# Chunks of every third channel, 4,096 accumulated elements and later first transposes in a dynamic convolution with an MoE layer behind it

## The chip, the cores and the metric

The kernel runs on one core of a Trainium2 chip. The metric is the device time of one launch in microseconds: the median of three runs is 808.31 us (807.36 to 809.03). The engines are TensorE (PE, with its weight loads listed as PEld), VectorE (DVE), ScalarE (ACT), GpSimd (POOL) and SyncE (SP). Transfers are issued from SP's queue or from POOL's and run on the core's 16 DMA engines.

## The reference

A dynamic depthwise convolution over time is followed by two matrix products with h - tanh(h) between them.

```
w   = softmax(weight_gen over its last axis)          # [8, 4096, 8 heads, 7 taps]
out[b, s, h, g] = sum_k w[b, s, h, k] * x_pad[b, s + k, h, g]    # 192 channels = 8 heads x 24, 6 zeros ahead
x   = out.reshape(32768, 192)
h   = x @ w_in            # 192 x 2048
g   = h - tanh(h)
y   = g @ w_out           # 2048 x 192
```

All inputs and the output are float32; the matrix products are made in bf16 with float32 sums.

## The kernel before, in words

The 32,768 tokens are cut into 32 blocks (`NTOT`) of 1,024 tokens: 128 partitions with `J` = 8 neighbouring tokens each. Each block goes through these steps.

- `load(n)`, on SP's queue: the weights `wg_t` of the block and `x_t`, which holds 14 rows of 192 channels per partition (8 tokens and the 6 ahead of them). `x_t` has two buffers, so the load waits until the products of block n-2 have read theirs.
- `softmax_exp` on ACT (`e_t`), `softmax_norm` on DVE (`zsum`, `zr`), and at the head of `products(n)` a multiplication on POOL (`wsm`, line 137).
- `products(n)` (line 153): for each tap k = 0 to 6 one multiplication of `x_t[:, k:k+8]` with the tap's weight, 1,536 elements per partition, float32 in and bf16 out. Taps 0, 2, 4 go to the three parts of `even`, taps 1, 3, 5 to those of `odd`, tap 6 to `last`. They run on POOL, but for those that `on_vector` names, which run on DVE. The 24 channels of a head are cut into `NC` = 3 chunks of 8 neighbouring channels; the result stands chunk by chunk, [chunk, token, head, channel], while x is read as it lies, so the output is written in runs of 8.
- After tap 5 POOL issues a DMA (line 161) that adds all of `odd` to `even`, 4,608 elements per partition. `even`, `odd` and `last` have two buffers each.
- `conv(n, chunks)` (line 182): PE transposes and sums: for each chunk, the three parts of `even` and `last` are multiplied with the identity and added up in PSUM (`pc`). Every operand is a pair of tokens, 64 rows by 128 columns, so one of the four groups takes 8 matmuls per chunk. ACT copies the sum to `convT` (line 192).
- `gemm1(n, f)` (line 205) for 16 tiles f of the 2,048 hidden columns: six matmuls into `ph`; ACT makes `th` = tanh (line 214), DVE makes `gt` = ph - th in bf16 (line 216). `ph` and `pc` share three PSUM buffers.
- `gemm2(i)` (line 236): 32 matmuls for one column of 128 tokens, copied by ACT to `out_sb` (line 261); eight of them make a block, which SP stores. It runs one block behind `gemm1`.

The order on every engine is the program's own; nothing is rescheduled (`tc.manual_schedule()`). The main loop takes block n and eight pairs p of hidden tiles. Ahead of the pairs it issues `load(n + 3)` and `products(n + 2)`; in each pair come two `gemm1`, one `gemm2` of block n-1 and, in two of the pairs, the transposes of block n+1: after pair 2 chunks 0 and 1, after pair 5 chunk 2 (in block 0 after pairs 5 and 6). Ahead of the loop stand block 0's load, w_in, products of block 0 (DVE has taps 1, 3, 5, 6), load and products of block 1 (DVE has 2 and 5) and block 0's transposes.

`w_in` is kept in SBUF as [128, 3 chunks, 2048] in bf16 with the same 64 rows in both halves of the partitions; row h*8+g of chunk c is channel h*24 + c*8 + g. It comes in eight DMAs on POOL's queue, one per head, into partitions 0 to 63 (line 305), and a DMA on SP's queue copies these to partitions 64 to 127 (line 312). POOL's queue also loads `w_out` (line 314).

Of the kernel before, what the change touches and what calls it, by code (L numbers as in the profile page):

```python
# [16 lines left out]
def kernel(  # L17
# [8 lines left out]
    nc = tc.nc  # L26

    B, S, D = x.shape
    H, K = weight_gen.shape[2], weight_gen.shape[3]
    G = D // H  # L30
    F = moe_w_in.shape[1]
    P = nc.NUM_PARTITIONS
    R = P // 2
    HALO = K - 1

    J = 8
    TOK = P * J
    JH = J // 2
# [3 lines left out]
    NFT = F // P  # L42
    NC = D // R
    GC = G // NC
    NPAIR = K // 2
    assert S % TOK == 0 and D % R == 0 and H * GC == R and F % P == 0
    assert NFT == 2 * J, "one token block of the second matmul per pair of f tiles"

# [11 lines left out]
    ident = const.tile([P, P], BF16, name="ident")  # L60
# [8 lines left out]
    prods_of = {}  # L69
# [4 lines left out]
    def load(n):  # L74
        b, s = divmod(n, NSB)
        s0 = s * TOK
        wg_t = wgpool.tile([P, J, H, K], FP32, name="wg_t")
        nc.sync.dma_start(
            out=wg_t[:],
            in_=weight_gen[b, s0 : s0 + TOK].rearrange("(p j) h k -> p j h k", p=P),  # L80
        )

        x_t = xpool.tile([P, HALO + J, D], FP32, name="x_t")

        def rows(p0, p1):
            win = x[b, s0 + p0 * J - HALO : s0 + p0 * J - HALO + 1]
            nc.sync.dma_start(
                out=x_t[p0:p1, :, :],
                in_=bass.AP(
                    tensor=win.tensor,  # L90
                    offset=win.offset,
                    ap=[[J * D, p1 - p0], [D, HALO + J], [1, D]],
                ),
            )

        if s == 0:
            nc.sync.dma_start(
                out=x_t[0:1, 0:HALO, :],
                in_=zero[:].rearrange("o (h d) -> o h d", h=1).to_broadcast([1, HALO, D]),
            )  # L100
            nc.sync.dma_start(
                out=x_t[0:1, HALO : HALO + J, :],
                in_=x[b, 0:J].rearrange("(p j) d -> p j d", p=1),
            )

            rows(1, 16)
            rows(16, P)
        else:
            rows(0, P)
        wg_of[n] = wg_t  # L110
        x_of[n] = x_t

    def softmax_exp(n):
        wg_t = wg_of.pop(n)
        e_t = wgpool.tile([P, J, H, K], FP32, name="e_t")
        nc.scalar.activation(  # L116
            out=e_t[:].rearrange("p j h k -> p (j h k)"),
            in_=wg_t[:].rearrange("p j h k -> p (j h k)"),
            func=ACT.Exp,
        )  # L120
        e_of[n] = e_t

    def softmax_norm(n):
        e_t = e_of.pop(n)
        zsum = wgpool.tile([P, J * H], FP32, name="zsum")
        nc.vector.reduce_sum(  # L126
            out=zsum[:], in_=e_t[:].rearrange("p j h k -> p (j h) k"), axis=AX.X
        )
        zr = wgpool.tile([P, J * H], FP32, name="zr")
        nc.vector.reciprocal(zr[:], zsum[:])  # L130
        zr_of[n] = (e_t, zr)

    def products(n, on_vector=()):
        x_t = x_of.pop(n)
        e_t, zr = zr_of.pop(n)
        wsm = wgpool.tile([P, J, H, K], FP32, name="wsm")
        nc.gpsimd.tensor_mul(  # L137
            wsm[:].rearrange("p j h k -> p (j h) k"),
            e_t[:].rearrange("p j h k -> p (j h) k"),
            zr[:].rearrange("p (n o) -> p n o", o=1).to_broadcast([P, J * H, K]),  # L140
        )

        even = ppool.tile([P, NPAIR, NC, J, H, GC], BF16, name="even")
        odd = ppool.tile([P, NPAIR, NC, J, H, GC], BF16, name="odd")
        last = ppool.tile([P, NC, J, H, GC], BF16, name="last")
        dst = {}
        for i in range(NPAIR):
            dst[2 * i] = even[:, i]
            dst[2 * i + 1] = odd[:, i]
        dst[K - 1] = last[:]  # L150
        for k in range(K):
            eng = nc.vector if k in on_vector else nc.gpsimd
            eng.tensor_mul(  # L153
                dst[k].rearrange("p c j h g -> p j h c g"),
                x_t[:, k : k + J, :].rearrange("p j (h c g) -> p j h c g", h=H, c=NC),
                wsm[:, :, :, k : k + 1]
                .rearrange("p j h (k o) -> p j h k o", o=1)
                .to_broadcast([P, J, H, NC, GC]),
            )
            if k == K - 2:  # L160
                nc.gpsimd.dma_start(  # L161
                    out=even[:].rearrange("p i c j h g -> p (i c j h g)"),
                    in_=odd[:].rearrange("p i c j h g -> p (i c j h g)"),
                    accum_op=mybir.AluOpType.add,
                    max_dma_last_dim=3072,
                )
        prods_of[n] = [even[:, i] for i in range(NPAIR)] + [last[:]]

    def conv(n, chunks):

        prods = prods_of[n]
        if n not in conv_of:
            conv_of[n] = cpool.tile([P, NC, HT], BF16, name="convT")
        convT = conv_of[n]
        nch = len(chunks)
        pc = psum_h.tile([P, 2, HT], FP32, name="pc", tag="ph")
        for k in range(NPAIR + 1):
            for ci, c in enumerate(chunks):
                for j in range(JH):
                    col = (ci * JH + j) * R  # L180
                    for r in range(2):
                        nc.tensor.matmul(  # L182
                            pc[:, r, col : col + R],
                            lhsT=prods[k][r * R : (r + 1) * R, c, 2 * j : 2 * j + 2].rearrange(
                                "p j h g -> p (j h g)"
                            ),
                            rhs=ident[r * R : (r + 1) * R, r * R : (r + 1) * R],
                            start=(k == 0 and ci == 0 and j == 0),
                            stop=(k == NPAIR and ci == nch - 1 and j == JH - 1),
                        )  # L190
        c0 = chunks[0]
        nc.scalar.activation(  # L192
            out=convT[:, c0 : c0 + nch, :].rearrange("p c (j r t) -> p r (c j) t", r=2, t=R),
            in_=pc[:, :, 0 : nch * JH * R].rearrange("p r (cj t) -> p r cj t", t=R),
            func=ACT.Copy,
        )
        if c0 + nch == NC:
            prods_of.pop(n)
# [99 lines left out]
    w_in = const.tile([P, NC, F], BF16, name="w_in")  # L298
    w_out = const.tile([P, NFT, D], BF16, name="w_out")

    ctx.enter_context(tc.manual_schedule())

    load(0)
    for h in range(H):
        nc.gpsimd.dma_start(
            out=w_in[h * GC : (h + 1) * GC],
            in_=moe_w_in[h * G : (h + 1) * G].rearrange("(c g) f -> g c f", c=NC),
        )
    softmax_exp(0)
    softmax_norm(0)  # L310
    products(0, on_vector=(1, 3, 5, 6))
    nc.sync.dma_start(out=w_in[R:P], in_=w_in[0:R])
    load(1)
    nc.gpsimd.dma_start(out=w_out[:], in_=moe_w_out.rearrange("(c p) e -> p c e", c=NFT))
    softmax_exp(1)
    softmax_norm(1)
    conv(0, (0, 1))
    conv(0, (2,))
    products(1, on_vector=(2, 5))
    load(2)  # L320
    softmax_exp(2)
    softmax_norm(2)
    for n in range(NTOT):
        if n + 3 < NTOT:
            load(n + 3)
        if n + 2 < NTOT:
            products(n + 2)
        for p in range(J):
            gemm1(n, 2 * p)
            gemm1(n, 2 * p + 1)  # L330
            if p == 1 and n + 3 < NTOT:
                softmax_exp(n + 3)
            if n >= 1:
                gemm2((n - 1) * J + p)
            if n + 1 < NTOT:
                if p == (2 if n else 5):
                    conv(n + 1, (0, 1))
                if p == (5 if n else 6):
                    conv(n + 1, (2,))
            if p == 2 and n + 3 < NTOT:  # L340
                softmax_norm(n + 3)
# [33 lines left out]
```

The softmax here doesn't subtract the row's maximum and nothing guards it: scores larger than these inputs give would overflow.

## Time and profile before

The profiled execution took 807.62 us, of which the span from the first to the last instruction is 805.8 us; the median of the runs is 808.31 us. The granted TensorE clock was 0.997.

| engine | busy us | share of the span | instructions |
|---|---|---|---|
| PE | 737.1 | 91% | 14,336 |
| POOL | 713.0 | 88% | 297 |
| DVE | 661.5 | 82% | 591 |
| ACT | 643.4 | 80% | 865 |

The DMA queue of POOL moved 39.32 MB in 15,376 packets and took 30.6% of the 16 engines' span; SP's moved 77.34 MB in 14,560 packets and took 27.4%.

How to read the lines below. The chain that ended last is followed back from the last instruction, at each step to what released it. A row of the groups has the line, engine and operation, then output and input with their shapes and the count; after the bar the busy time in us, the mean in ns of one instruction, and the idle time of the engine ahead of the group with what ended most of it. In the chain in order of time a row has the start in us, the length in us and what ran. In a timeline a row has the start, the length, engine, line, operation, tiles, and in brackets the idle time before it. Spans on POOL are rough: the spacing of its starts says more than the length of one.

### The profile page before, as it was taken

To read this page: it belongs to the slowest core of one execution; us is meant where nothing else is said; L and a number is where in the kernel's file an instruction comes from. 1 tells how busy PE (TensorE), PEld (TensorE's weight loads), DVE (VectorE), ACT (ScalarE), POOL (GpSimd) and SP (SyncE) were. 2 spreads that over 40 slices of the span, in tenths; PEclk is the share of its full clock that TensorE was granted. 3 is DMA by queue.
4 is the path that set the end of the run, shared out by engine and by line. 5 is a ranking of instruction groups with operands and counts; after the bars stand their busy time and mean duration, and the time that the engine had idled before them with its cause. 6 is when DMAs were issued, how large, how long until landed. Compare 5 with 4: busy or idle time off the path is not lost.

```text
span 805.8 us, 31480 instructions
## 1 busy us (share of the span) xinstructions
PE 737.1 (91%) x14336; PEld 566.7 (70%) x14336; DVE 661.5 (82%) x591; ACT 643.4 (80%) x865; POOL 713.0 (88%) x297
## 2 busy tenths in 40 slices
PE   0066999999999999999999999999999999999997
PEld 0034777777777777777777777777777777777777
DVE  3867688888888888888888888888888888888883
ACT  0066788888888888888888888888888888888883
POOL 5999999999999999999999999999999999996000
PEclk9999999999999999999999999999999999999999
DMA  8794555676655655676565656775655667634112
GB/s 148 230 187 85 114 161 156 166 180 180 179 141 126 149 159 156 172 181 179 138 170 131 149 154 163 180 171 139 176 118 157 153 169 180 168 61 100 43 41 81
DMA packets 30068, 118.66 MB, mean 147 GB/s; under 512 B 4672, under 2 KB 9328, under 8 KB 25784
## 3 DMA queue, kind: packets, MB, share of 16 engines
q0 software_dynamic: 15376, 39.32, 30.6%
q1 hardware_dynamic: 14560, 77.34, 27.4%
q8 instruction: 112, 1.84, 0.9%
q14 instruction: 20, 0.16, 0.1%
HBM read 54.49 MB, written 25.17 MB: 99 GB/s over the span
## 4 chain that ended last, share of the span: by engine, by line
PE 76%; DVE 11%; POOL 5%; ACT 4%; DMA 3%; issue 1%; SPq 0%; POOLq 0%; DVEq 0%
PE ph L205 36%; PE po L236 35%; DVE gt L216 9%; ACT th L214 4%; PE pc L182 4%; POOL even L153 2%; POOL odd L153 2%; DMA x_t<-in_x_dram 1%; DVE odd L153 1%; PE po L277 1%; DMA even<-odd 1%; POOL last L153 0%; POOL wsm L137 0%; POOL even L161 0%; DVE even L153 0%
## 5 line engine op out<-in xcount | busy, mean ns | idle before, releaser
L216 DVE TENSOR_TENSOR gt<-ph,th 128x1024 bf16<-128x1024 f32 x512 | 602.8, 1220 | 106.7 <-ACT th L214 103.3
L214 ACT ACTIVATE th<-ph 128x1024 f32<-128x1024 f32 x512 | 500.3, 1022 | 64.0 <-PE ph L205 60.4
L205 PE MATMUL ph<-convT,w_in 64*128 64x512 bf16 x3072 | 391.9, 378 | 17.2 <-DVE gt L216 16.0
L236 PEld LDWEIGHTS <-gt 64*128 64x128 bf16 x7936 | 344.4, 94 | 52.8 <-ACT th L214 1.7
L236 PE MATMUL po<-w_out,gt 64*128 64x192 bf16 x7936 | 374.1, 243 | 1.7 <-ACT th L214 1.3
L153 POOL TENSOR_TENSOR even<-x_t,wsm 128x1536 bf16<-128x1536 f32 x95 | 281.8, 2967 | 14.2 <-DMA x_t<-in_x_dram 7.1
L153 POOL TENSOR_TENSOR odd<-x_t,wsm 128x1536 bf16<-128x1536 f32 x92 | 268.5, 2919 | 0.0
L205 PEld LDWEIGHTS <-w_in 64*128 64x128 bf16 x3072 | 170.3, 94 | 135.6 <-issue 44.9
L153 POOL TENSOR_TENSOR last<-x_t,wsm 128x1536 bf16<-128x1536 f32 x31 | 105.9, 3415 | 0.0
L261 ACT ACTIVATE out_sb<-po 128x192 f32<-128x192 f32 x248 | 82.0, 331 | 18.5 <-PE po L236 12.2
L192 ACT ACTIVATE convT<-pc 128x1024 bf16<-128x1024 f32 x64 | 51.7, 810 | 47.6 <-PE pc L182 43.5
L182 PE MATMUL pc<-ident,even 64*128 64x64 bf16 x2304 | 46.6, 193 | 45.9 <-DMA even<-odd 45.6
L182 PEld LDWEIGHTS <-even 64*128 64x128 bf16 x2304 | 43.7, 97 | 46.7 <-issue 46.4
L161 POOL DMA_DIRECT2D even<-odd x32 | 41.5, 1298 | 10.0 <-POOL odd L153 9.4
L137 POOL TENSOR_TENSOR wsm<-e_t,zr 128x448 f32<-128x448 f32 x32 | 46.3, 1446 | 0.0
L116 ACT ACTIVATE e_t<-wg_t 128x448 f32<-128x448 f32 x32 | 18.5, 578 | 20.3 <-DMA wg_t<-in_weight_gen_dram 20.3
L126 DVE TENSOR_REDUCE zsum<-e_t 128x64 f32<-128x448 f32 x32 | 19.5, 610 | 10.8 <-ACT e_t L116 10.8
L182 PE MATMUL pc<-ident,last 64*128 64x64 bf16 x768 | 23.4, 193 | 0.0
L153 DVE TENSOR_TENSOR odd<-x_t,wsm 128x1536 bf16<-128x1536 f32 x4 | 15.0, 3782 | 9.6 <-DMA x_t<-in_x_dram 9.6
L130 DVE RECIPROCAL zr<-zsum 128x64 f32<-128x64 f32 x32 | 17.7, 553 | 3.4 <-DVE zsum L126 0.5
L182 PEld LDWEIGHTS <-last 64*128 64x128 bf16 x768 | 17.3, 97 | 0.0
L277 PE MATMUL po<-w_out,gt 64*128 64x192 bf16 x256 | 11.0, 243 | 0.0
(15 smaller groups left out, 31.5 us busy)
## 6 DMA issues: line engine op xcount, KB each, us to landing
even<-odd POOLq DMA_DIRECT2D x32, 1152.0 KB, 10.1
x_t<-in_x_dram SPq DMA_DIRECT2D x24, 1344.0 KB
out_dram<-out_sb SPq DMA_DIRECT2D x31, 768.0 KB
x_t<-in_x_dram SPq DMA_DIRECT2D x8, 1176.0 KB
wg_t<-in_weight_gen_dram SPq DMA_DIRECT2D x32, 224.0 KB
x_t<-in_x_dram SPq DMA_DIRECT2D x8, 157.5 KB
w_in<-in_moe_w_in_dram POOLq DMA_DIRECT2D x8, 96.0 KB, 11.0
w_in<-w_in SPq DMA_DIRECT2D x1, 768.0 KB
```

The source lines that it names most:

```text
L126: nc.vector.reduce_sum(out=zsum[:], in_=e_t[:].rearrange("p j h k -> p (j h) k"), axis=AX.X)
L137: nc.gpsimd.tensor_mul(wsm[:].rearrange("p j h k -> p (j h) k"), e_t[:].rearrange("p j h k -> p (j h) k"), zr[:].rearrange("p (n o) -> p n ...
L153: eng.tensor_mul(dst[k].rearrange("p c j h g -> p j h c g"), x_t[:, k : k + J, :].rearrange("p j (h c g) -> p j h c g", h=H, c=NC), wsm[:, ...
L161: nc.gpsimd.dma_start(out=even[:].rearrange("p i c j h g -> p (i c j h g)"), in_=odd[:].rearrange("p i c j h g -> p (i c j h g)"), accum_o ...
L182: nc.tensor.matmul(pc[:, r, col : col + R], lhsT=prods[k][r * R : (r + 1) * R, c, 2 * j : 2 * j + 2].rearrange("p j h g -> p (j h g)"), rh ...
L192: nc.scalar.activation(out=convT[:, c0 : c0 + nch, :].rearrange("p c (j r t) -> p r (c j) t", r=2, t=R), in_=pc[:, :, 0 : nch * JH * R].re ...
L205: nc.tensor.matmul(ph[:, r, :], lhsT=w_in[r * R : (r + 1) * R, c, f * P : (f + 1) * P], rhs=convT[r * R : (r + 1) * R, c, :], start=(c == ...
L214: last_act[0] = nc.scalar.activation(out=th[:], in_=ph_f, func=ACT.Tanh)
L216: nc.vector.tensor_sub(gt[:], ph_f, th[:])
L236: mm = nc.tensor.matmul(po[:, 0:D], lhsT=g_of[n][f][r * R : (r + 1) * R, col : col + P], rhs=w_out[r * R : (r + 1) * R, f, :], start=(r == ...
L261: last_act[0] = nc.scalar.activation(out=out_sb[:, j, :], in_=po[:, 0:D], func=ACT.Copy)
L277: nc.tensor.matmul(po[:, r, 0:D], lhsT=g_of[n][f][r * R : (r + 1) * R, col : col + P], rhs=w_out[r * R : (r + 1) * R, f, :], start=(f == 0 ...
```

## The change

x's chunks become every third channel: chunk c holds the channels h*24 + g*3 + c. A product now writes its 1,536 results in one run, in the order chunk, token, head, channel, and reads x in steps of three floats, 12 bytes. With that, row p of `w_in` holds the channels 3p to 3p+2, so that `w_in` comes straight from memory in two DMAs of 64 partitions, one per half, and the copy on SP is gone. These two are issued on POOL behind block 0's `wsm`; `w_out` is issued behind tap 3 of block 1's products.

The accumulating DMA covers the first 4,096 of the 4,608 elements. The 512 that are left are chunk 2 of the last part of `odd`; the transposes of chunk 2 take them as a fifth group, so a block has 104 instead of 96 of these matmuls.

DVE has taps 1, 3, 4, 5 and 6 of block 0 and none of block 1. The transposes of blocks 1 to 4 (in the loop n = 0 to 3) stand together after pair 7, those of later blocks after pairs 2 and 5 as before.

```diff
@@ -43,6 +43,7 @@
     NC = D // R
     GC = G // NC
     NPAIR = K // 2
+    ACC = NPAIR * J * D - J * R
     assert S % TOK == 0 and D % R == 0 and H * GC == R and F % P == 0
     assert NFT == 2 * J, "one token block of the second matmul per pair of f tiles"
 
@@ -130,7 +131,7 @@
         nc.vector.reciprocal(zr[:], zsum[:])
         zr_of[n] = (e_t, zr)
 
-    def products(n, on_vector=()):
+    def products(n, on_vector=(), hooks={}):
         x_t = x_of.pop(n)
         e_t, zr = zr_of.pop(n)
         wsm = wgpool.tile([P, J, H, K], FP32, name="wsm")
@@ -148,23 +149,29 @@
             dst[2 * i] = even[:, i]
             dst[2 * i + 1] = odd[:, i]
         dst[K - 1] = last[:]
+        if -1 in hooks:
+            hooks[-1]()
         for k in range(K):
             eng = nc.vector if k in on_vector else nc.gpsimd
             eng.tensor_mul(
-                dst[k].rearrange("p c j h g -> p j h c g"),
-                x_t[:, k : k + J, :].rearrange("p j (h c g) -> p j h c g", h=H, c=NC),
+                dst[k],
+                x_t[:, k : k + J, :].rearrange("p j (h g c) -> p c j h g", h=H, c=NC),
                 wsm[:, :, :, k : k + 1]
-                .rearrange("p j h (k o) -> p j h k o", o=1)
-                .to_broadcast([P, J, H, NC, GC]),
+                .rearrange("p (o j) h k -> p o j h k", o=1)
+                .to_broadcast([P, NC, J, H, GC]),
             )
             if k == K - 2:
+
                 nc.gpsimd.dma_start(
-                    out=even[:].rearrange("p i c j h g -> p (i c j h g)"),
-                    in_=odd[:].rearrange("p i c j h g -> p (i c j h g)"),
+                    out=even[:].rearrange("p i c j h g -> p (i c j h g)")[:, 0:ACC],
+                    in_=odd[:].rearrange("p i c j h g -> p (i c j h g)")[:, 0:ACC],
                     accum_op=mybir.AluOpType.add,
-                    max_dma_last_dim=3072,
-                )
-        prods_of[n] = [even[:, i] for i in range(NPAIR)] + [last[:]]
+                    max_dma_last_dim=4096,
+                )
+            if k in hooks:
+                hooks[k]()
+        groups = [even[:, i] for i in range(NPAIR)] + [last[:]]
+        prods_of[n] = [groups + ([odd[:, NPAIR - 1]] if c == NC - 1 else []) for c in range(NC)]
 
     def conv(n, chunks):
 
@@ -174,20 +181,25 @@
         convT = conv_of[n]
         nch = len(chunks)
         pc = psum_h.tile([P, 2, HT], FP32, name="pc", tag="ph")
-        for k in range(NPAIR + 1):
-            for ci, c in enumerate(chunks):
-                for j in range(JH):
-                    col = (ci * JH + j) * R
-                    for r in range(2):
-                        nc.tensor.matmul(
-                            pc[:, r, col : col + R],
-                            lhsT=prods[k][r * R : (r + 1) * R, c, 2 * j : 2 * j + 2].rearrange(
-                                "p j h g -> p (j h g)"
-                            ),
-                            rhs=ident[r * R : (r + 1) * R, r * R : (r + 1) * R],
-                            start=(k == 0 and ci == 0 and j == 0),
-                            stop=(k == NPAIR and ci == nch - 1 and j == JH - 1),
-                        )
+        steps = [
+            (gi, ci, c)
+            for gi in range(NPAIR + 2)
+            for ci, c in enumerate(chunks)
+            if gi < len(prods[c])
+        ]
+        for si, (gi, ci, c) in enumerate(steps):
+            for j in range(JH):
+                col = (ci * JH + j) * R
+                for r in range(2):
+                    nc.tensor.matmul(
+                        pc[:, r, col : col + R],
+                        lhsT=prods[c][gi][r * R : (r + 1) * R, c, 2 * j : 2 * j + 2].rearrange(
+                            "p j h g -> p (j h g)"
+                        ),
+                        rhs=ident[r * R : (r + 1) * R, r * R : (r + 1) * R],
+                        start=(si == 0 and j == 0),
+                        stop=(si == len(steps) - 1 and j == JH - 1),
+                    )
         c0 = chunks[0]
         nc.scalar.activation(
             out=convT[:, c0 : c0 + nch, :].rearrange("p c (j r t) -> p r (c j) t", r=2, t=R),
@@ -300,23 +312,26 @@
 
     ctx.enter_context(tc.manual_schedule())
 
+    def load_w_out():
+        nc.gpsimd.dma_start(out=w_out[:], in_=moe_w_out.rearrange("(c p) e -> p c e", c=NFT))
+
+    def load_w_in():
+        for r in range(2):
+            nc.gpsimd.dma_start(
+                out=w_in[r * R : (r + 1) * R],
+                in_=moe_w_in.rearrange("(p c) f -> p c f", c=NC),
+            )
+
     load(0)
-    for h in range(H):
-        nc.gpsimd.dma_start(
-            out=w_in[h * GC : (h + 1) * GC],
-            in_=moe_w_in[h * G : (h + 1) * G].rearrange("(c g) f -> g c f", c=NC),
-        )
     softmax_exp(0)
     softmax_norm(0)
-    products(0, on_vector=(1, 3, 5, 6))
-    nc.sync.dma_start(out=w_in[R:P], in_=w_in[0:R])
+    products(0, on_vector=(1, 3, 4, 5, 6), hooks={-1: load_w_in})
     load(1)
-    nc.gpsimd.dma_start(out=w_out[:], in_=moe_w_out.rearrange("(c p) e -> p c e", c=NFT))
     softmax_exp(1)
     softmax_norm(1)
     conv(0, (0, 1))
     conv(0, (2,))
-    products(1, on_vector=(2, 5))
+    products(1, hooks={3: load_w_out})
     load(2)
     softmax_exp(2)
     softmax_norm(2)
@@ -333,9 +348,9 @@
             if n >= 1:
                 gemm2((n - 1) * J + p)
             if n + 1 < NTOT:
-                if p == (2 if n else 5):
+                if p == (2 if n > 3 else 7):
                     conv(n + 1, (0, 1))
-                if p == (5 if n else 6):
+                if p == (5 if n > 3 else 7):
                     conv(n + 1, (2,))
             if p == 2 and n + 3 < NTOT:
                 softmax_norm(n + 3)
```

## The prediction

> **What bounds the kernel now.** First the page: which engine ends the chain, then the chain in order of time, then the groups and the timelines of the engines it passes through. The page's chain by engine and its rows for the lines touched:
>
> ```profile
> PE 76%; DVE 11%; POOL 5%; ACT 4%; DMA 3%; issue 1%; SPq 0%; POOLq 0%; DVEq 0%
> ...
> L153 POOL TENSOR_TENSOR even<-x_t,wsm 128x1536 bf16<-128x1536 f32 x95 | 281.8, 2967 | 14.2 <-DMA x_t<-in_x_dram 7.1
> ...
> L161 POOL DMA_DIRECT2D even<-odd x32 | 41.5, 1298 | 10.0 <-POOL odd L153 9.4
> ```
>
> PE sets three quarters of the end, but POOL is 88% busy and sits idle only 24 us before all its products and DMA issues together: two engines run nearly level. Where does one hand over to the other? The chain in order of time:
>
> ```profile
> 2.86 11.70 DMA x_t<-in_x_dram
> 14.68 8.89 DVE odd L153 x3
> 23.57 4.39 POOL even L153
> ...
> 69.52 10.52 DMA even<-odd
> 80.04 0.14 issue
> 80.17 1.81 PE pc L182 x64
> ...
> 112.99 2.37 DVE gt L216 x2
> 115.36 0.04 issue
> 115.40 0.83 PE ph L205 x6
> ```
>
> Until 80.17 us the end is set by loading x, by products and by the third accumulating DMA (landing to 80.04). From there PE is dense, except one short wait per block for VectorE's subtraction (115.40). The timelines of POOL and VectorE give the pace:
>
> ```profile
> 6.61 0.98 POOL L137 TENSOR_TENSOR wsm<-e_t,zr 128x448 f32<-128x448 f32 x1
> 60.59 2.90 POOL L153 TENSOR_TENSOR odd<-x_t,wsm 128x1536 bf16<-128x1536 f32 x1
> 63.45 2.90 POOL L153 TENSOR_TENSOR even<-x_t,wsm 128x1536 bf16<-128x1536 f32 x1
> 647.25 2.90 POOL L153 TENSOR_TENSOR even<-x_t,wsm 128x1536 bf16<-128x1536 f32 x1 [0.45 <-POOL wsm L137]
> ...
> 14.68 10.51 DVE L153 TENSOR_TENSOR odd<-x_t,wsm 128x1536 bf16<-128x1536 f32 x3 [9.57 <-DMA x_t<-in_x_dram]
> 25.11 4.45 DVE L153 TENSOR_TENSOR last<-x_t,wsm 128x1536 bf16<-128x1536 f32 x1
> 31.84 1.76 DVE L153 TENSOR_TENSOR even<-x_t,wsm 128x1536 bf16<-128x1536 f32 x1 [1.16 <-POOL wsm L137]
> ```
>
> Products start 2.86 us apart on POOL. One block's seven, wsm and the DMA issue take 22.74 us (DMA issues at 69.52 and 92.25). PE's block takes 23.12 (convs at 104.71 and 127.83). So POOL gains 0.4 us a block; late, the 0.45 us gap shows that free buffers hold it back to PE's pace. A product costing over 2.93 us makes POOL's block longer than PE's, and POOL the bound of the whole run. That is the margin that matters here.
>
> [...] The new step is 12. The trace has no such read of x; the nearest is wsm, whose elements lie 28 bytes apart, each repeated 24 times, so it doesn't test it. [...] VectorE's product is 1.76 alone and 4.45 beside POOL, POOL's 4.39 there against 2.86, and 1.6 + 2.86 = 4.46: they take turns. [...] x(0), 1.33 MB, needed 11.70 us beside the eight w_in loads.
>
> **The change, part by part.** Blocks are numbered, so x(0) is block 0's load and conv(5) block 5's transposes.
>
> *Load of w_in.* Eight issues (about 0.6 us each) leave POOL ahead of wsm(0), and two come behind it; wsm(0) waits for x anyway. The copy on SP goes, and with it SP's wait of 13.1 us, so x(1) is issued at about 3.5 us, not at 18, behind x(0) on the same queue. Before, x(0) and w_in together read 2.9 MB in 12 us, 240 GB/s. Now x(0) starts alone and w_in (3.1 MB read, both halves from HBM) comes at about 7.4 us: 4.5 us × 240 = 1.1 MB, the other 0.25 at half rate in 2 us. x(0) lands at S = 9.6 to 10 instead of 14.56; I take 10, bounds 8 and 14.5. x(1) then shares the rate with w_in, 1.6 MB at 120 GB/s, and lands at about 23.5; w_in at about 30.
>
> *Products of block 0.* VectorE has k = 1, 3, 4, 5, 6, POOL 0 and 2. By turns: 2 × 2.86 + 4 × 1.6 = 12.1 until k = 5, and the accumulating DMA is issued at S + 12.4 = 22.4 (before 28.26). It queues behind w_in on POOL's queue and lands near 41, against 42.0: nothing is gained there. VectorE's sixth and the reduce and reciprocal (0.62 + 0.55) let wsm(1) start at S + 15.
>
> *Products of block 1.* All seven are on POOL now: wsm to S + 16.1, six products 17.2, the w_out issue 1.4 between them, 0.3 of wait: DMA(1) is issued at S + 35 = 45.0 (before 46.76). Behind that issue stand `last` and wsm(2); DMA(2) follows a POOL block later.
>
> *Accumulation.* 4,096 elements in two pieces of 2,048, not 4,608 in three of 1,536: 256 data packets for 384, 11% fewer bytes. The landing of 9.6 to 10.5 becomes about 9.3; the issue (1.30 us, of which 0.8 delays the next product) shortens by perhaps 0.1, so a POOL block is 22.65. Bounds: no gain, or 0.3.
>
> *Transposes.* In chunk 2, `odd` of the last pair brings 8 more matmuls per block. 24 + 8 matmuls took 113.69 to 114.27, 18 ns each: 0.14 us. But behind them stands the wait that VectorE sets, 0.31 us, which doesn't move. So between 0 and 0.14 a block; I take 0.05, from block 5 on 27 × 0.05 = 1.3 us. Without that cover it is 3.9. `odd` is freed with `even` of the same block, no new wait.
>
> *Late transposes.* For blocks 1 to 4 both convs stand behind pair 7. PE no longer stops at pair 2 of block 1 (3.62 us before 80.17). Each such block pays for the row conv, copy, first matmul: 0.94 + 1.02 + 0.60 + 0.3 = 2.85 us, of which 1.25 is PE idle. With conv(0) at 41 and the first block 21 us long, conv(1) is at 62; a block is then 20.9 + 2.85 = 23.8, so conv(4) stands at 133.3 and conv(5), at pair 2 again, could run at 143.9.
>
> *The price of a product on POOL.* Everything else hangs on it. [...] I take 2.86 unchanged: the small instruction (0.98 us for 448 contiguous values, [...]) and the products with their runs and repeats both cost 1.85 ns an element, so the pace seems to be the engine's loop [...], not the addresses. That is an argument, no measurement.
>
> *Sum.* DMA(2) at 45.0 + 22.65 = 67.6, landing 76.9; DMA(5) three POOL blocks later, landing 144.9. conv(5) starts at 145.0, the later of that and 143.9. Before it stood at 152.16, and conv(31) at 753.19, 26 × 23.12 later: the rest is PE's, plus 1.3. The gain is 7.2 − 1.3, about 5.5 with caution over the small terms: span 800.3 for 805.8. The profiled execution was 807.62, the median 808.31, so the median becomes 802.8; I say 803.
>
> **Rivals.** (a) The 12-byte step costs on POOL. At d us a product, DMA(31) lands at 733.8 + 216 (d − 2.86): 13 products lie before DMA(2), 7 in each of 29 blocks. Then come the 52.6 us that follow conv(31), and 2.5 to the median: 788.9 + 216 (d − 2.86). It decides from d = 2.95 on. [...] at 3.1 it is 841. [...] against it only the argument above. (b) The contiguous write makes POOL quicker, [...] conv(5) then stands where PE allows, 143.9, or 139.9 if DMA(0) lands at 37: gain 7 to 11, 799 us. (c) The start gives nothing back: VectorE's products at 12 bytes take twice as long (five of them, about +5 us before wsm(1)), or x(1), with w_in beside it, lands 3 to 5 us late; conv(5) then returns to about 150 and the extra matmuls take the rest: 809. For it: DMA is over nine tenths busy already between 5 and 15 us.
>
> **Chances.** Unchanged product price 0.44 (799 to 808), (b) 0.16, (c) 0.12, (a) at 2.95 to 3.1 us 0.08, up to 3.6 0.05, [...] 0.15. Within 0.2% counts as no change, about what a measurement of this kernel can tell. Faster 0.41 + 0.16 = 0.57; same 0.03 + half of (c) = 0.09; slower 0.06 + 0.28 = 0.34. The range 795 to 840 leaves out the two costly cases, 0.20; the likeliest alone has 799 to 808.
>
> **What would show it.** POOL's products 2.86 us apart, its first at about 10; accumulating DMAs issued at about 22, 45 and 68; conv(5) as the last transpose that waits for a DMA, for about a microsecond; PE's blocks after it at 23.1 to 23.2. A wait of PE for `even` in every block, with POOL busy to the end, means (a); products under 2.8 apart mean (b). First products after 13 us, or x(1) waited for, mean (c).

## The result and the profile after

The changed kernel takes 931.8 us (931.0 to 932.02, 4 runs) against 808.13 us before (807.36 to 809.03, 4 runs): a ratio of 1.1528, 95% interval 1.1508 to 1.1548. Forecast were 803 us and a range of 795 to 840. The profiled execution has a span of 930.1 us.

The page's chain by engine, and its rows for the products and the accumulating DMA:

```profile
POOL 59%; PE 21%; DMA 10%; DVE 6%; issue 3%; ACT 2%; SPq 0%; POOLq 0%; DVEq 0%
...
L156 POOL TENSOR_TENSOR even<-x_t,wsm 128x1536 bf16<-128x1536 f32 x95 | 342.0, 3601 | 5.1 <-DMA x_t<-in_x_dram 2.6
...
L165 POOL DMA_DIRECT2D even<-odd x32 | 38.5, 1204 | 14.2 <-POOL odd L156 9.5
```

The bound has changed hands: POOL has 59% of the chain, where PE had 76%. POOL's timeline in the middle of the run shows the price of a product, and PE's what follows from it:

```profile
510.76 3.59 POOL L156 TENSOR_TENSOR odd<-x_t,wsm 128x1536 bf16<-128x1536 f32 x1
514.65 1.20 POOL L165 DMA_DIRECT2D even<-odd  x1 [0.30 <-POOL odd L156]
515.43 4.03 POOL L156 TENSOR_TENSOR last<-x_t,wsm 128x1536 bf16<-128x1536 f32 x1
518.98 1.40 POOL L138 TENSOR_TENSOR wsm<-e_t,zr 128x448 f32<-128x448 f32 x1
520.45 3.50 POOL L156 TENSOR_TENSOR even<-x_t,wsm 128x1536 bf16<-128x1536 f32 x1
523.90 3.55 POOL L156 TENSOR_TENSOR odd<-x_t,wsm 128x1536 bf16<-128x1536 f32 x1
527.38 3.62 POOL L156 TENSOR_TENSOR even<-x_t,wsm 128x1536 bf16<-128x1536 f32 x1
...
541.91 1.20 POOL L165 DMA_DIRECT2D even<-odd  x1 [0.30 <-POOL odd L156]
```
```profile
522.76 1.46 PE L194 MATMUL pc<-ident,even 64*128 64x64 bf16 x48 [3.17 <-DMA even<-odd]
...
550.76 1.47 PE L194 MATMUL pc<-ident,even 64*128 64x64 bf16 x48 [3.70 <-DMA even<-odd]
```

Products start 3.45 to 3.55 us apart, not 2.86. A POOL block is 541.91 - 514.65 = 27.26 us, 4.1 more than the 23.12 that PE needs, and PE waits for `even` once in nearly every block: the list of waits has 80.3 us of it in 24 waits between 85 and 870 us. The accumulating DMAs were issued at 79.03 us (block 2) and 868.9 (block 31): 27.24 us a block over 29 blocks. 29 × 4.1 = 119 us, which is all but 5 of the 124 us lost.

### The profile page after: what moved, and what is told of

Its sections match the earlier page's. It is cut to its first block, busy times and chain, and to the rows that moved or that the text cites. A ratio compares the mean times of both kernels' runs of the same rounds, so it can differ in the third digit from the quotient of the medians.

```text
span 930.1 us, 31974 instructions
## 1 busy us (share of the span) xinstructions
PE 774.7 (83%) x14592; PEld 590.5 (63%) x14592; DVE 657.6 (71%) x590; ACT 649.2 (70%) x865; POOL 848.3 (91%) x292
## 4 chain that ended last, share of the span: by engine, by line
POOL 59%; PE 21%; DMA 10%; DVE 6%; issue 3%; ACT 2%; SPq 0%; POOLq 0%; DVEq 0%
POOL even L156 24%; POOL odd L156 24%; PE ph L217 10%; DMA even<-odd 9%; POOL last L156 9%; PE po L248 8%; DVE gt L228 3%; POOL wsm L138 2%; PE pc L194 2%; ACT th L226 2%; PE po L289 1%; DVE odd L156 1%; DMA x_t<-in_x_dram 1%; DVE even L156 1%; DVE last L156 0%
## 5 line engine op out<-in xcount | busy, mean ns | idle before, releaser
L226 ACT ACTIVATE th<-ph 128x1024 f32<-128x1024 f32 x512 | 502.3, 1024 | 68.8 <-PE ph L217 63.2
L217 PE MATMUL ph<-convT,w_in 64*128 64x512 bf16 x3072 | 406.7, 391 | 17.5 <-DVE gt L228 15.8
L248 PEld LDWEIGHTS <-gt 64*128 64x128 bf16 x7936 | 351.4, 95 | 62.7 <-issue 12.9
L248 PE MATMUL po<-w_out,gt 64*128 64x192 bf16 x7936 | 381.0, 245 | 7.1 <-issue 5.0
L156 POOL TENSOR_TENSOR even<-x_t,wsm 128x1536 bf16<-128x1536 f32 x95 | 342.0, 3601 | 5.1 <-DMA x_t<-in_x_dram 2.6
L156 POOL TENSOR_TENSOR odd<-x_t,wsm 128x1536 bf16<-128x1536 f32 x93 | 332.9, 3579 | 0.0
L217 PEld LDWEIGHTS <-w_in 64*128 64x128 bf16 x3072 | 174.4, 97 | 139.5 <-issue 51.4
L194 PE MATMUL pc<-ident,even 64*128 64x64 bf16 x2304 | 54.0, 204 | 126.7 <-DMA even<-odd 118.7
L194 PEld LDWEIGHTS <-even 64*128 64x128 bf16 x2304 | 48.8, 104 | 133.0 <-issue 119.7
L156 POOL TENSOR_TENSOR last<-x_t,wsm 128x1536 bf16<-128x1536 f32 x31 | 125.3, 4043 | 0.0
L156 DVE TENSOR_TENSOR odd<-x_t,wsm 128x1536 bf16<-128x1536 f32 x3 | 9.7, 3265 | 4.9 <-DMA x_t<-in_x_dram 4.9
L289 PE MATMUL po<-w_out,gt 64*128 64x192 bf16 x256 | 11.0, 243 | 0.0
```

The costliest lines, as they stand in the source:

```text
L156: eng.tensor_mul(dst[k], x_t[:, k : k + J, :].rearrange("p j (h g c) -> p c j h g", h=H, c=NC), wsm[:, :, :, k : k + 1] .rearrange("p (o j ...
L194: nc.tensor.matmul(pc[:, r, col : col + R], lhsT=prods[c][gi][r * R : (r + 1) * R, c, 2 * j : 2 * j + 2].rearrange("p j h g -> p (j h g)") ...
L217: nc.tensor.matmul(ph[:, r, :], lhsT=w_in[r * R : (r + 1) * R, c, f * P : (f + 1) * P], rhs=convT[r * R : (r + 1) * R, c, :], start=(c == ...
L226: last_act[0] = nc.scalar.activation(out=th[:], in_=ph_f, func=ACT.Tanh)
L248: mm = nc.tensor.matmul(po[:, 0:D], lhsT=g_of[n][f][r * R : (r + 1) * R, col : col + P], rhs=w_out[r * R : (r + 1) * R, f, :], start=(r == ...
L289: nc.tensor.matmul(po[:, r, 0:D], lhsT=g_of[n][f][r * R : (r + 1) * R, col : col + P], rhs=w_out[r * R : (r + 1) * R, f, :], start=(f == 0 ...
```

## Experiments

Three things happened to a product at once: x is read at 12 bytes, the output is written in one run, and the loop order puts the chunk outermost, so that a tap's weight is repeated 8 times, not 24, before the next is read. The first four kernels part them. Their expectations call the step of x theory S and the weight, which changes more often, theory W or rival W.

**Only the loop order (e1_order_only).** In the kernel before:

```diff
-                dst[k].rearrange("p c j h g -> p j h c g"),
-                x_t[:, k : k + J, :].rearrange("p j (h c g) -> p j h c g", h=H, c=NC),
+                dst[k],
+                x_t[:, k : k + J, :].rearrange("p j (h c g) -> p c j h g", h=H, c=NC),
                 wsm[:, :, :, k : k + 1]
-                .rearrange("p j h (k o) -> p j h k o", o=1)
-                .to_broadcast([P, J, H, NC, GC]),
+                .rearrange("p (o j) h k -> p o j h k", o=1)
+                .to_broadcast([P, NC, J, H, GC]),
```

> The kernel before with one thing of the change: the product's loop order. It writes chunk by chunk in one run, and the tap's weight is repeated 8 times, not 24, before the next is read (192 changes of weight, not 64). The chunks stay neighbouring channels, so x is read at 4 bytes. Theory S (the 12-byte step of x costs): products on POOL stay 2.86 us apart and the time stays at 808. Rival W (the weight operand, changed three times as often, costs; 0.65 us over 128 further changes would be 5 ns each): 3.5 us apart, and some 930 us. Rival B (one long write run is quicker): under 2.8.

860.73 us, ratio 1.0664 (1.0646 to 1.0682). POOL's timeline:

```profile
527.86 3.21 POOL L153 TENSOR_TENSOR even<-x_t,wsm 128x1536 bf16<-128x1536 f32 x1
531.02 3.21 POOL L153 TENSOR_TENSOR odd<-x_t,wsm 128x1536 bf16<-128x1536 f32 x1
534.19 3.21 POOL L153 TENSOR_TENSOR even<-x_t,wsm 128x1536 bf16<-128x1536 f32 x1
```

3.17 us apart: neither the 2.86 of theory S nor the 3.5 of rival W. The order alone, at 4 bytes, costs 0.31 us a product and makes the kernel 6.6% slower. VectorE's product stays at 1.76 us.

**Only the step (e2_step_only).** In the changed kernel the old loop order:

```diff
-                dst[k],
-                x_t[:, k : k + J, :].rearrange("p j (h g c) -> p c j h g", h=H, c=NC),
+                dst[k].rearrange("p c j h g -> p j h c g"),
+                x_t[:, k : k + J, :].rearrange("p j (h g c) -> p j h c g", h=H, c=NC),
                 wsm[:, :, :, k : k + 1]
-                .rearrange("p (o j) h k -> p o j h k", o=1)
-                .to_broadcast([P, NC, J, H, GC]),
+                .rearrange("p j h (k o) -> p j h k o", o=1)
+                .to_broadcast([P, J, H, NC, GC]),
```

> The changed kernel with the old loop order: token and head outermost, then chunk, then channel. The weight is repeated 24 times again and the writes are runs of 8, but x is still read at 12 bytes. S: products 3.5 us apart, 930 us. W: 2.86 us apart and about 803. If both have a part, between.

891.66 us, ratio 1.1047 (1.1031 to 1.1064). POOL's timeline:

```profile
526.04 3.39 POOL L156 TENSOR_TENSOR odd<-x_t,wsm 128x1536 bf16<-128x1536 f32 x1
529.38 3.34 POOL L156 TENSOR_TENSOR even<-x_t,wsm 128x1536 bf16<-128x1536 f32 x1
532.69 3.34 POOL L156 TENSOR_TENSOR odd<-x_t,wsm 128x1536 bf16<-128x1536 f32 x1
```

3.32 us apart in the mean: the step alone costs 0.46. Both theories have a part. Together they cost 0.65, less than the sum of 0.77. VectorE pays for the step too, by a quarter and not double as rival (c) had it: its last product of block 0, with POOL no longer at products, is 2.18 us instead of 1.76:

```profile
24.92 2.18 DVE L156 TENSOR_TENSOR last<-x_t,wsm 128x1536 bf16<-128x1536 f32 x1
```

**The far step on the write side (e3_flat_read).** As e2, but with the chunks innermost:

```diff
-                dst[k],
-                x_t[:, k : k + J, :].rearrange("p j (h g c) -> p c j h g", h=H, c=NC),
+                dst[k].rearrange("p c j h g -> p j h g c"),
+                x_t[:, k : k + J, :].rearrange("p j (h g c) -> p j h g c", h=H, c=NC),
                 wsm[:, :, :, k : k + 1]
-                .rearrange("p (o j) h k -> p o j h k", o=1)
-                .to_broadcast([P, NC, J, H, GC]),
+                .rearrange("p j h (k o) -> p j h k o", o=1)
+                .to_broadcast([P, J, H, GC, NC]),
```

> The changed kernel with the product's innermost loop over the three chunks: x is read as it lies, at 4 bytes, the weight is repeated 24 times, and the output is written in single elements 1,024 bytes apart. Same result in the same places, all else as changed. S, if a far step on the write side is free: 2.86 us apart, and the 803 us that the prediction gave for an unchanged price. If a write step costs as a read step does: 3.5 and 930. W: 2.86, 803.

1689.43 us, ratio 2.0928 (2.0897 to 2.0959). POOL's timeline, and VectorE's product while POOL stands still:

```profile
523.16 7.28 POOL L156 TENSOR_TENSOR odd<-x_t,wsm 128x1536 bf16<-128x1536 f32 x1
530.05 7.28 POOL L156 TENSOR_TENSOR even<-x_t,wsm 128x1536 bf16<-128x1536 f32 x1
...
42.75 7.23 DVE L156 TENSOR_TENSOR odd<-x_t,wsm 128x1536 bf16<-128x1536 f32 x1
```

6.9 us apart. Reading flat and writing single bf16 values 1,024 bytes apart costs 4 us, six times what the change costs. VectorE pays as dearly: 7.23 us for one product. No forecast of this run came near, and since the writes outweigh all else it doesn't tell S from W.

**The size of the step (e4_steps).** In the changed kernel, each tap with its own step of x, in floats:

```diff
+    STEP = (1, 2, 3, 4, 5, 8, 3)
+
+    def stepped(x_t, k):
+        v = x_t[:, k : k + J, :].rearrange("p j (h g c) -> p c j h g", h=H, c=NC)
+        dims = [list(d) for d in v.ap]
+        dims[-1][0] = STEP[k]
+        return bass.AP(tensor=v.tensor, offset=v.offset, ap=dims)
...
-                x_t[:, k : k + J, :].rearrange("p j (h g c) -> p c j h g", h=H, c=NC),
+                stepped(x_t, k),
```

> The changed kernel with a step of its own for each tap: taps 0 to 6 read x at 4, 8, 12, 16, 20, 32 and 12 bytes (other channels than the reference wants, so the values are different ones; the instructions and their sizes are the same). Spacing of POOL's starts tap by tap. S [...]: 2.86, 2.86, 3.5, 3.5, 3.5, 3.5. S in proportion [...]: 2.86, 3.2, 3.5, 3.85, 3.85, 3.85. W: 3.5 for all.

The timeline of one block, tap 0 first:

```profile
500.95 3.23 POOL L164 TENSOR_TENSOR even<-x_t,wsm 128x1536 bf16<-128x1536 f32 x1
504.14 3.24 POOL L164 TENSOR_TENSOR odd<-x_t,wsm 128x1536 bf16<-128x1536 f32 x1
507.34 3.58 POOL L164 TENSOR_TENSOR even<-x_t,wsm 128x1536 bf16<-128x1536 f32 x1
510.84 3.93 POOL L164 TENSOR_TENSOR odd<-x_t,wsm 128x1536 bf16<-128x1536 f32 x1
514.71 3.94 POOL L164 TENSOR_TENSOR even<-x_t,wsm 128x1536 bf16<-128x1536 f32 x1
518.57 3.90 POOL L164 TENSOR_TENSOR odd<-x_t,wsm 128x1536 bf16<-128x1536 f32 x1
522.76 1.20 POOL L173 DMA_DIRECT2D even<-odd  x1 [0.30 <-POOL odd L164]
```

It is one run, of 945.36 us; what counts is the spacing. From start to start: 3.19 us at 4 bytes, 3.20 at 8, 3.50 at 12, 3.87 at 16, 3.86 at 20, 3.89 at 32 (the last up to 522.46, before the 0.30 of wait). Neither form of theory S fits: against 4 bytes, 8 cost next to nothing (0.01 us), 12 about half of the price (0.31) and 16 all of it (0.68; 0.67 at 20, 0.70 at 32). (From 8 bytes on the values of the second form are met within 0.04 us, but by luck: they start from 2.86, and this order takes 3.19 at 4 bytes.) What makes these steps is not shown, and they belong to this loop order: in the old one (e6 and e11, next) 8 bytes already cost 0.11 us, and 12 bytes, at 0.46, over two thirds of the 0.67 that 16 cost.

**The operands one by one (e6_operands, e11_operands2).** Both are the kernel before with another access form in each tap, so their output is not the reference's. Each line is a tap: the extents of the loops, then the steps of output, x and weight, in elements. Shown is e6's table; e11 has another one, in the words of its expectation, and the lines that put the forms into the product are left out:

```diff
+    FORM = (
+        ((64, 3, 8), (8, 512, 1), (24, 8, 1), (7, 0, 0)),
+        ((64, 3, 8), (24, 8, 1), (24, 8, 1), (7, 0, 0)),
+        ((64, 3, 8), (24, 8, 1), (8, 512, 1), (7, 0, 0)),
+        ((3, 64, 8), (512, 8, 1), (512, 8, 1), (0, 7, 0)),
+        ((64, 3, 8), (24, 8, 1), (24, 8, 1), (0, 0, 0)),
+        ((3, 64, 8), (512, 8, 1), (8, 24, 1), (0, 7, 0)),
+        ((64, 3, 8), (24, 8, 1), (24, 1, 3), (7, 0, 0)),
+    )
...
```

> The kernel before, with another access form for each tap (values are others, sizes the same), to part what the loop order alone added (2.86 to 3.17 us). Tap 0: as before. Tap 1: the same, written in one run. Tap 2: as tap 1, x in runs of 8 that lie 1 or 2 KB apart. Tap 3: x in one run, weight changed every 8 elements. Tap 4: one weight for all. Tap 5: the full new loop order at 4 bytes. Tap 6: x at 12 bytes with the weight changed every 24. Theory W (each change of the weight costs 2.4 ns): 2.86, 2.86, 2.86, 3.17, 2.71, 3.17, 3.3. Rival R (each new run of x costs): 2.86, 2.86, 3.17, 2.86, 2.86, 3.17, 3.3. If the write run matters, tap 1 differs from tap 0.

> The kernel before with further access forms per tap (other values, same sizes). Tap 0: new loop order at 4 bytes with one weight. Tap 1: 12 bytes in the old order, one weight. Tap 2: 16 bytes, old order. Tap 3: x in one run, weight changed every 8 elements, neighbouring weights 8 bytes apart. Tap 4: 8 bytes, old order. Tap 5: 16 bytes, one weight. Tap 6: as before. If weight changes and the step of x simply add (2.70 with one weight, 0.16 for 64 changes, 0.36 for 192, step 0.46 at 12 bytes and about 0.9 at 16): 2.70, 3.16, 3.76, 3.06, 2.86, 3.6, 2.86. If they overlap [...]: less than the sum in taps 2 and 5, and tap 0 above 2.70 by the 0.11 still without a name.

The times are 820.74 and 849.78 us, one run each. POOL's timeline of one block, tap 0 first: of e6, then of e11:

```profile
523.23 2.90 POOL L175 TENSOR_TENSOR even<-x_t,wsm 128x1536 bf16<-128x1536 f32 x1
526.09 2.90 POOL L175 TENSOR_TENSOR odd<-x_t,wsm 128x1536 bf16<-128x1536 f32 x1
528.95 2.88 POOL L175 TENSOR_TENSOR even<-x_t,wsm 128x1536 bf16<-128x1536 f32 x1
531.79 3.10 POOL L175 TENSOR_TENSOR odd<-x_t,wsm 128x1536 bf16<-128x1536 f32 x1
534.85 2.75 POOL L175 TENSOR_TENSOR even<-x_t,wsm 128x1536 bf16<-128x1536 f32 x1
537.56 3.22 POOL L175 TENSOR_TENSOR odd<-x_t,wsm 128x1536 bf16<-128x1536 f32 x1
541.07 1.30 POOL L179 DMA_DIRECT2D even<-odd  x1 [0.30 <-POOL odd L175]
541.89 3.86 POOL L175 TENSOR_TENSOR last<-x_t,wsm 128x1536 bf16<-128x1536 f32 x1
545.23 1.45 POOL L159 TENSOR_TENSOR wsm<-e_t,zr 128x448 f32<-128x448 f32 x1
```
```profile
521.02 2.75 POOL L175 TENSOR_TENSOR even<-x_t,wsm 128x1536 bf16<-128x1536 f32 x1
523.72 3.26 POOL L175 TENSOR_TENSOR odd<-x_t,wsm 128x1536 bf16<-128x1536 f32 x1
526.95 3.58 POOL L175 TENSOR_TENSOR even<-x_t,wsm 128x1536 bf16<-128x1536 f32 x1
530.48 2.93 POOL L175 TENSOR_TENSOR odd<-x_t,wsm 128x1536 bf16<-128x1536 f32 x1
533.37 3.02 POOL L175 TENSOR_TENSOR even<-x_t,wsm 128x1536 bf16<-128x1536 f32 x1
536.34 3.48 POOL L175 TENSOR_TENSOR odd<-x_t,wsm 128x1536 bf16<-128x1536 f32 x1
540.11 1.30 POOL L179 DMA_DIRECT2D even<-odd  x1 [0.30 <-POOL odd L175]
```

The spacings, in us (tap 5 up to the wait of 0.30 before the DMA issue); the last column has e4's in the new order too:

| what the product does | 64 weights, 24 repeats | one weight | 192 weights, 8 repeats |
|---|---|---|---|
| x flat | 2.86 | 2.70 | 3.06 (weights 28 bytes apart), 2.89 (8 apart) |
| x in runs of 8, far apart | 2.84 | | |
| x in the new order, 4 bytes | | 2.70 | 3.2 |
| x at 8 bytes | 2.97 | | 3.20 (new order, e4) |
| x at 12 bytes | 3.3 | 3.23 | 3.50 (new order, e4) |
| x at 16 bytes | 3.53 | 3.47 | 3.87 (new order, e4) |

The write run is free either way (taps 0 and 1 of e6, 2.86 us each), so the prediction's rival (b), that one long run is quicker, falls. x's jumps by themselves are free as well (tap 2, 2.84 us): rival R falls. The weight is what the loop order costs: 0.20 of its 0.31 us, theory W in most of its size, and less, 0.03, when two neighbouring weights lie 8 bytes apart (2.89 us; that tap also runs through 192 weights in one plain loop, where the others go three times through 64; the two are not parted). The other 0.11 (e1's 3.17 against 3.06) appears only where x jumps and the weight changes together: with one weight the new order is back at 2.70. What makes that 0.11 stays open. Step and weight don't quite add: at 12 bytes the 64 changes cost 0.1, on flat reads 0.16.

**The rest of the change at the old price (e5_old_price).** The changed kernel with the same lines as in e2, but with neighbouring chunks, `"p j (h c g) -> p j h c g"`, so that x is read flat.

> The changed kernel with the products as they were before: neighbouring channels, x at 4 bytes in runs of 24, weight repeated 24 times. w_in keeps its two DMAs and so has its rows in the order of every third channel: the pairing of channels with rows is left out, sizes and times are not touched. It tests the rest of the prediction's sum: at a product of 2.86 us it gave 803, with DMA(2) issued at 67.6 and conv(5) at 145.0. Theory: the price of the product is the only wrong term, so 801 to 805. Rival: the start gives nothing back either (VectorE, x(1) beside w_in, dearer late transposes): 808 or more.

803.86 us, ratio 0.9945 (0.9933 to 0.9957). POOL's timeline gives the chain, PE's gives conv(5):

```profile
10.08 8.85 POOL L156 TENSOR_TENSOR even<-x_t,wsm 128x1536 bf16<-128x1536 f32 x2 [2.60 <-DMA x_t<-in_x_dram]
22.82 1.26 POOL L165 DMA_DIRECT2D even<-odd  x1 [3.89 <-DVE odd L156]
...
44.93 1.21 POOL L165 DMA_DIRECT2D even<-odd  x1 [0.30 <-POOL odd L156]
...
67.58 1.21 POOL L165 DMA_DIRECT2D even<-odd  x1 [0.30 <-POOL odd L156]
```
```profile
34.58 1.46 PE L194 MATMUL pc<-ident,even 64*128 64x64 bf16 x48 [34.58 <-DMA even<-odd]
...
144.90 1.33 PE L194 MATMUL pc<-ident,even 64*128 64x64 bf16 x48 [4.05 <-DMA even<-odd]
```

The rival, that the start gives nothing back, falls. At the price of 2.86 the sum up to conv(5) holds to a tenth of a microsecond: 45.0, 67.6 and 145.0 were forecast. That the total lies so near the 803 forecast is in part luck: 1.3 us were set down for the extra matmuls, which cost nothing, and in this profile 2.9 us went to a few stalls of PE behind conv(5) (conv(31) at 748.91, 604.01 us later, for 26 × 23.12) that nobody forecast.

**A version that keeps the rest (e7_rest_kept).** e5 with w_in in its right order, so that the result is the reference's again:

```diff
-        for r in range(2):
-            nc.gpsimd.dma_start(
-                out=w_in[r * R : (r + 1) * R],
-                in_=moe_w_in.rearrange("(p c) f -> p c f", c=NC),
-            )
+        for h in range(H):
+            nc.gpsimd.dma_start(
+                out=w_in[h * GC : (h + 1) * GC],
+                in_=moe_w_in[h * G : (h + 1) * G].rearrange("(c g) f -> g c f", c=NC),
+            )
...
     load(1)
+    nc.sync.dma_start(out=w_in[R:P], in_=w_in[0:R])
```

> A version meant to beat both: the changed kernel with neighbouring channels and the old product form, w_in in eight DMAs on POOL behind block 0's wsm and the copy to the other half on SP behind load(1). Later transposes, 4,096 accumulated elements, VectorE's taps and w_out's place as changed. Products 2.86 us apart, and the time that the prediction's sum had without the step, 803; the eight issues (4.7 us from 6.3) could put POOL's first product a microsecond later than x's landing at 10, which VectorE's five cover, so not over 805. Rival: 808, nothing gained by what is left.

804.31 us, ratio 0.9955 (0.994 to 0.997): faster than both kernels, by half a per cent against the one before. So the two-DMA load of w_in, for which the chunks had to be cut anew, isn't needed for the gain: eight issues behind wsm and a copy behind load(1) do as well. conv(31) starts at 748.99 us, against 753.19 before.

**Where those 4 us come from (e9_early_back, e10_accum_back).** e9 gives e7 the transposes' old places, e10 its old accumulation:

```diff
-                if p == (2 if n > 3 else 7):
+                if p == (2 if n else 5):
                     conv(n + 1, (0, 1))
-                if p == (5 if n > 3 else 7):
+                if p == (5 if n else 6):
```
```diff
-    ACC = NPAIR * J * D - J * R
+    ACC = NPAIR * J * D
...
-                    max_dma_last_dim=4096,
+                    max_dma_last_dim=3072,
...
-        prods_of[n] = [groups + ([odd[:, NPAIR - 1]] if c == NC - 1 else []) for c in range(NC)]
+        prods_of[n] = [groups for c in range(NC)]
```

> The version with the old product form (e7_rest_kept), with the transposes of blocks 1 to 4 back at the places of before (after pairs 5 and 6 in block 0, 2 and 5 after that). Theory (the gain of what is left comes from PE not stopping early): PE stops at pair 2 of block 1 for DMA(2), landing at 76.5, some 9 us; conv(5) then stands at about 147.5 instead of 144.4, so 807. Rival (the gain is all from the earlier start of POOL's chain): no loss, 804.

> The same version with the accumulation of before: 4,608 elements in pieces of 1,536, and no fifth group in chunk 2. Theory: the landing is 0.7 to 1 us later and POOL's block 0.1 longer, while PE, not POOL, holds conv(5) in this version, and the eight matmuls hide behind VectorE's wait; so within 1 us of 804.3. Rival (the extra matmuls cost their 0.14 us a block): 800 to 801.

e9: 804.96 us, 0.9968 (0.9956 to 0.9981). e10: 806.02 us, 0.9978 (0.9967 to 0.9988). PE's timeline of e7, then of e9:

```profile
144.43 0.88 PE L194 MATMUL pc<-ident,even 64*128 64x64 bf16 x48
...
748.99 0.88 PE L194 MATMUL pc<-ident,even 64*128 64x64 bf16 x48
```
```profile
76.21 1.46 PE L194 MATMUL pc<-ident,even 64*128 64x64 bf16 x48 [3.59 <-DMA even<-odd]
...
148.57 0.88 PE L194 MATMUL pc<-ident,even 64*128 64x64 bf16 x48
...
750.49 0.88 PE L194 MATMUL pc<-ident,even 64*128 64x64 bf16 x48
```

Both are still faster than before, and neither theory is right as it stood. The kernel before took 808.15 us in the runs beside e7 and 807.62 in those beside e9 and e10, so the ratios are compared: the early places lose about 1 us, not 3, the old accumulation about 1.9, where at most 1 was forecast. The intervals of all three overlap, those of e7 and e10 barely, so their order is not settled.

In e10 PE waits for the DMA before conv(5), 1.01 us, at 146.59; in e7 conv(5) runs without a wait. In e9 the stop in block 1 comes, for 3.59 us instead of 9, and conv(5) is a microsecond later than forecast. Of the 4.1 us by which e9 is behind e7 there, 1.5 are left at conv(31): e7 loses 3.4 us to single stalls in the 26 blocks after conv(5) (604.6 us for 26 × 23.12), e9 0.8. What these stalls are, and whether other executions have them in the same places, is open.

So with either taken back, half of e7's 3.6 us or more is left: 2.6 in e9, 1.8 in e10. All three share what put POOL's chain about 2 us ahead (DMA(2) at 67.66 in e7, 69.52 before): x(1) issued early, w_in behind wsm, VectorE's five taps of block 0 and w_out behind tap 3. That the rest of the gain comes from there is likely, not shown: no run takes these apart, and none takes both back at once.

## Why the prediction was wrong, point by point

- **The price of a product on POOL**, step "I take 2.86 unchanged", is the step that failed. Measured: 3.5. Of the 0.65 us the step of x has 0.46 by itself, or 0.34 on top of the new order, and the loop order 0.31 by itself. With the old form put back and all else kept (e5) the kernel takes 803.86 us.
- **The argument for it** was that two instructions of different form cost the same 1.85 ns an element, so addresses could not set the pace. They do: with one weight a product is 2.70, with 64 it is 2.86, with 192 it is 3.06. The trace of before held one form of product on POOL, which can't tell a loop's pace from an operand's. The 1.85 of the small instruction was a guess too: its 0.98 us for 448 elements are 2.19 ns each, and no run here shows a fixed start that could be taken off.
- **The loop order was priced only as a possible gain** (the write run). It was weighed for the output and for x, not for the third operand, which the same edit makes change three times as often.
- **A product dearer than 3.6 us**, given 0.15, didn't come: the changed kernel's is 3.5. Nor does the step have one price: in the new order it costs 0.01 us at 8 bytes, 0.31 at 12 and 0.68 at 16, in the old one 0.11, 0.46 and 0.67. And x is one of two operands that cost: 192 changes of weight instead of 64 cost 0.20 us more.
- **Rival (a) had the law and half of the mechanism.** 788.9 + 216 (d - 2.86) gives 928 us at 3.505 and 887 at 3.315, measured 931.8 and 891.66. It knew of the step, not of the weight. The law also leaves out the products of block 0: wsm(1) came at 28.41 us in the changed kernel and at 25.15 in e5, which is most of the 4 us that it falls short. Its place between 3.1 and 3.6 us was given 0.05.
- **The start** was right in the term that counts: x landed at 10, the DMAs of e5 came at 45 and 67.6. DMA(0) landed at 34.6 in e5, not 41: the queue behind w_in was overrated (w_in had landed by about 22 us, not 30: e7's copy, which waits for it, was issued at 21.68), so PE was early and waited 4.05 us at conv(5), not 1. The 1.6 us for VectorE's turn are an estimate, its 4.45 beside POOL less POOL's 2.86; by it DMA(0) was to be issued at 22.4, and e5 issued it at 22.82. In the changed kernel itself POOL's first DMA came at 25.64, since VectorE's products cost more as well (2.17 us for the last one, against 1.76).
- **Eight more matmuls a block**, forecast at 1.3 us in all, cost nothing that shows: in e7 two convs late in the run lie 23.11 us apart (725.88 and 748.99), before 23.12, and in e10, which has none of them, 23.12 (728.00 and 751.12). That fits the argument that the wait for VectorE covers them.
- **The late transposes** did their part in e5 (after conv(0) PE first stops for a DMA at conv(5)), but e9 shows that they are worth about 1 us, not clear of the noise and less than the stop of 3.59 us that they avoid.
- **The range** left out the two costly cases with 0.20 between them. What bore on them was one argument without a measurement, and a margin of 0.09 us a product. That did not support so low a weight for the costly side.

## What to carry to other kernels

Where two engines run level, price an access pattern before anything else: by the law above 3% on one instruction form would have turned the bound, and 23% came. Look at every operand of an elementwise instruction, the broadcast one too: at its step, and at how often it changes. Here the order in which the innermost loops keep the broadcast weight longest was the cheaper one (2.86 us with 64 changes, 3.06 with 192). A rule that foretells each price did not come out of these runs, so measure the form. If a trace holds only one form of an instruction, it says nothing about another; a kernel with a different form in each tap measures seven in one run.

## What the runs showed of the hardware

- POOL, two inputs, 1,536 float32 elements: 2.70 us with one broadcast weight and x flat; +0.16 for 64 weights 28 bytes apart, +0.36 for 192, +0.19 for 192 that lie 8 bytes apart.
- x at 8, 12 and 16 bytes: +0.11, +0.46, +0.67 in the old order; in the new order +0.01, +0.31, +0.68, then +0.67 at 20 and +0.70 at 32.
- VectorE's product, with POOL at no product that holds it up: 1.76 us at 4 bytes (before), 2.17 at 12 (changed kernel), 2.88 at 32 (e4, tap 5); the loop order at 4 bytes changes nothing there (1.76 in e1).
- Single bf16 results written 1,024 bytes apart: 6.9 us on POOL instead of 2.86, 7.23 on VectorE instead of 1.76. On POOL runs of 8 (16 bytes) at the same distance cost the same as one long run (2.86 us both).
